# Loading the last head of W_o as sixteen loads of 15, 14, 13 ... 1 partitions instead of one load of 128

## The chip, the cores and the metric

The kernel runs on one NeuronCore of one Trainium2 chip. The metric is the device time of one execution in microseconds (us). The kernel before takes 659.15 us, the median of three runs that lie between 659.08 and 659.29. The profile is of one execution of the same program.

## The reference, cut to what matters

Two blocks follow each other for a batch of B = 2, one token each, width D = 512, in bf16: attention over a cache of 8192 positions with 32 heads of 128, and a gated layer of width F = 1376.

```python
h  = x + A(layernorm(x))          # A: q = x @ wq; softmax(q k^T / sqrt(128)) v; ... @ wo
h2 = h + B(layernorm(h))          # B: relu(x @ W_gate) * (x @ W_up) @ W_down
# k_cache, v_cache: (2, 32, 8192, 128)   wq: (512, 4096)   wo: (4096, 512)
# W_gate, W_up: (512, 1376)   W_down: (1376, 512)
```

The two caches are 256 MiB, the weights about 12 MiB. Each byte is read once and used for little arithmetic.

## The kernel before, in words

The cache is walked in steps of four heads of one batch entry; the last four heads are done in two steps of two heads, called p0 and p1 (in the code `steps[Q+1]` and `steps[Q+2]`). A step loads 8 MiB of keys and 8 MiB of values (half of that in p0 and p1) into three rotating buffers of the on-chip memory, `bufs[0]` to `bufs[2]`, in the trace `tile`. VectorE multiplies the keys by the query and sums them by halves (`products` L375, `scores` L393 and L395), TensorE and ScalarE take a share of the positions (`scores_pe`, L340 to L367, and `act_sums`, L381), and TensorE multiplies the exponentials with the values (`values` L446, `values_cols` L469).

All large loads are issued by SyncE (SP) in the order of the code, which is written out by hand. The tail of that order is: the values of p0; W_o's first set (`load_set(0)`, 2 MiB, L567); the values of p1 (4 MiB, L165); W_o's other three sets (1 MiB, 512 KiB and 256 KiB, L567); W_o's head 30 (128 KiB, L589); W_o's head 31 (128 KiB, L590); W_gate and W_up (1376 KiB each, L612); then W_down in seven loads, three of 32 partitions with 32 KiB each (L616) and four of 128 partitions with 640, 384, 128 and 128 KiB (L621). The last DMA stores the result (L736). Buffer space that a load writes has to be free first, so most issues carry a wait for the engine that read the old contents.

There is a second wait on each issue. The framework gives every DMA one of eight completion counters, in turn, in the order of issue. Before a counter is used again, SP waits until the DMA that used it last has landed completely. As SP issues in order, an issue waits for the DMA eight places before it, and everything behind it in the program of SP waits as well. In the program of the kernel before, the places at the tail are these (the number is the place in SP's own order):

```
34 values p0      35 W_o set 0     36 values p1     37 W_o set 1 (1 MiB)
38 W_o set 2      39 W_o set 3     40 W_o head 30   41 W_o head 31
42 W_gate         43 W_up          44-46 W_down 32-partition loads
47-50 W_down 128-partition loads   51 store
```

So W_gate (42) is issued when the values of p0 (34) have landed, W_up (43) when W_o's set 0 (35) has, the first small load of W_down (44) when the values of p1 (36) have.

After the last scores, TensorE multiplies the heads with W_o (`attend_set` L502; heads 30 and 31 by `attend`, L509), VectorE adds x (L659) and forms the second normalisation (L663 to L677), TensorE multiplies with W_gate and W_up (`through`, L686) and then with W_down (`down`, L719); `down` starts the result from the residual and goes through the eleven chunks of F, each of which needs its part of W_down. VectorE and ScalarE copy the result out (L734, L735), and SP stores it.

The functions that the edit touches:

Of the kernel before, what the change touches and what calls it, by code (L numbers as in the profile page):

```python
# [13 lines left out]
def _free(t, offset, dims):  # L14

    return bass.AP(tensor=t.tensor, offset=t.offset + offset, ap=[t.ap[0]] + [list(d) for d in dims])


def _dram(t, offset, dims):
    return bass.AP(tensor=t.tensor, offset=t.offset + offset, ap=[list(d) for d in dims])  # L20
# [3 lines left out]
def kernel(  # L24
# [13 lines left out]
    nc = tc.nc  # L38
    P = nc.NUM_PARTITIONS
    B, Sq, D = A_x.shape  # L40
    _, Hkv, Sk, Dh = A_k_cache.shape
    Hq = A_wq.shape[1] // Dh
# [26 lines left out]
    HM = 30  # L69
# [55 lines left out]
    wo = bufs[0][:, HALF:TILE]  # L125
# [61 lines left out]
    with tc.manual_schedule():  # L187

        for b, k, n in ((0, 0, 2), (0, 2, 2), (1, 0, 2), (1, 2, 1), (1, 3, 1)):
            nc.scalar.dma_start(  # L190
                out=xr[b:b + 1, k * P:(k + n) * P], in_=_dram(A_x, b * D + k * P, [[D, 1], [1, n * P]]),
# [10 lines left out]
            out=nscale, in_=nscale, compare_op=ALU.not_equal, fill=-SCALE,  # L202
# [5 lines left out]
            out=ident_f, in_=ident_f, compare_op=ALU.not_equal, fill=1.0,  # L208
# [4 lines left out]
            out=sel, in_=sel, compare_op=ALU.not_equal, fill=1.0,  # L213
# [9 lines left out]
            out=pick, in_=pick, compare_op=ALU.not_equal, fill=1.0,  # L223
# [24 lines left out]
        for g0 in range(0, NQ, 4):  # L248
            for n0 in range(NH * g0 * Dh, NH * (g0 + 4) * Dh, 4 * Dh):
                q_ps = ps2.tile([B, 4 * Dh], f32, tag="o")  # L250
                for c in range(KC):
                    nc.tensor.matmul(  # L252
                        out=q_ps, lhsT=xn[:, c, :], rhs=wq_sb[:, c, n0:n0 + 4 * Dh], start=(c == 0), stop=(c == KC - 1),
                    )
                nc.vector.tensor_copy(qrow[:, n0:n0 + 4 * Dh], q_ps)
            for b in range(B):
                r_ps = ps2.tile([P, 4, Dh], f32, tag="tp")
                for j in range(NH):
                    nc.tensor.matmul(
                        out=r_ps[j * (P // NH):(j + 1) * (P // NH)], lhsT=sel[:, b, 0:P // NH],  # L260
# [5 lines left out]
        for j in range(2):  # L266
            nc.tensor.matmul(
                out=r_ps[j * (P // 2):(j + 1) * (P // 2)], lhsT=sel[:, B - 1, :],
# [116 lines left out]
        def scores(s):  # L385

            scol = scols[s.i]
            width = Dh
            while width > 8:
                half = width // 2  # L390
                lo = _free(s.kt, s.na * Dh, [[Dh, s.nv - s.na], [1, half]])
                hi = _free(s.kt, s.na * Dh + half, [[Dh, s.nv - s.na], [1, half]])
                nc.vector.tensor_tensor(out=lo, in0=lo, in1=hi, op=ALU.add)  # L393
                width = half
            nc.vector.tensor_reduce(  # L395
                out=scol[:, s.na:s.nv], in_=_free(s.kt, s.na * Dh, [[Dh, s.nv - s.na], [1, 8]]), axis=AXIS.X, op=ALU.add,
            )
            pms[s.i] = small.tile([P, 1], f32, tag="pm", name="pm", bufs=2)
            nc.vector.tensor_reduce(out=pms[s.i], in_=scol, axis=AXIS.X, op=ALU.max)  # L399
# [187 lines left out]
        for k in range(1, len(SETS)):  # L587
            load_set(k)
        nc.sync.dma_start(out=wo[:, HM * D:(HM + 1) * D], in_=_dram(A_wo, HM * Dh * D, [[D, P], [1, D]]))  # L589
        nc.sync.dma_start(  # L590
            out=wo[:, (HM + 1) * D:Hq * D], in_=_dram(A_wo, (HM + 1) * Dh * D, [[P // 4 * D, 4], [D, P // 4], [1, D]]),
        )
        scores(p0)

        def first():
# [15 lines left out]
        for w, src in ((0, B_W_gate), (1, B_W_up)):  # L611
            nc.sync.dma_start(  # L612
                out=wgu[:, w].rearrange("p c f -> p (c f)"), in_=_dram(src, 0, [[KC * F, P], [1, KC * F]]),
            )
        for q0 in range(AGAIN, P, AGAIN):
            nc.sync.dma_start(  # L616
                out=wd_sb[q0:q0 + AGAIN, FC - 1, :], in_=_dram(B_W_down, (F - P + q0) * D, [[D, AGAIN], [1, D]]),
            )
        for f0, n in FSETS[:-1]:
# [10 lines left out]
            out=z2_ps, lhsT=ones, rhs=_free(zc, ((B - 1) * NQ + groups[Q][1]) * NH, [[1, nb]]), start=True, stop=True,  # L630
# [63 lines left out]
        for c in range(KC):  # L694
            nc.tensor.transpose(hT_ps[:, c, :], hb[:, c].rearrange("p k b -> p (k b)"), ident)
        nc.scalar.activation(
            out=hrow.rearrange("q (p c) -> q p c", c=KC), in_=hT_ps.rearrange("q c p -> q p c"), func=ACT.Copy,
# [9 lines left out]
            out=gate, in0=g_ps, scalar=0.0, in1=_free(rvar, 0, [[0, FC], [1, B]]), op0=ALU.max, op1=ALU.mult,  # L707
# [59 lines left out]
```

## Time and profile before

| what | from | value |
|---|---|---|
| median of three runs | times | 659.15 us (659.08 to 659.29) |
| the profiled execution's span | page | 657.5 us |
| median less span, which the span does not hold | worked out | 1.65 us |
| HBM read | page, part 3 | 281.05 MB, 427 GB/s over the span |
| busy share of VectorE / TensorE / ScalarE | page, part 1 | 85% / 54% / 19% |
| W_gate and W_up issued at | timeline of SP | 624.84 and 629.68 us |
| W_gate, issue to landing | page, part 6 | 22.8 us |
| last load of W_down, issue to landing | page, part 6 | 6.9 us |

The page gives no other time of the profiled execution than its span. Times in the views are counted from the start of the span. A row of SP in the timeline is the issue of a DMA, not its transfer: the transfer lies between the issue and the landing, and may wait behind older transfers. The transfers run on 16 DMA engines, and a DMA has landed when each engine that took part has reported; the trace also holds these reports one by one, and each engine's packets with their sizes and durations.

### The profile page before, as it was taken

To read this page: it belongs to the slowest core of one execution; us is meant where nothing else is said; L and a number is where in the kernel's file an instruction comes from. 1 tells how busy PE (TensorE), PEld (TensorE's weight loads), DVE (VectorE), ACT (ScalarE), POOL (GpSimd) and SP (SyncE) were. 2 spreads that over 40 slices of the span, in tenths; PEclk is the share of its full clock that TensorE was granted. 3 is DMA by queue.
4 is the path that set the end of the run, shared out by engine and by line. 5 is a ranking of instruction groups with operands and counts; after the bars stand their busy time and mean duration, and the time that the engine had idled before them with its cause. 6 is when DMAs were issued, how large, how long until landed. Compare 5 with 4: busy or idle time off the path is not lost.

```text
span 657.5 us, 5117 instructions
## 1 busy us (share of the span) xinstructions
PE 352.1 (54%) x2118; PEld 158.9 (24%) x2118; DVE 558.1 (85%) x252; ACT 123.6 (19%) x337; POOL 24.1 (4%) x36
## 2 busy tenths in 40 slices
PE   0730934809175380926539092552918458291997
PEld 0310311304022130312204031220403224030456
DVE  0599697988979799897979989796997969999982
ACT  0230030200203020030301103030210304201870
POOL 3080000000000000000000000000000000000020
PEclk9975775958778596877959687695968869686895
DMA  9999999999999999999999999999999999999997
GB/s 383 447 444 447 387 440 443 447 399 444 439 443 436 419 436 435 439 439 436 423 443 424 439 440 427 447 416 443 439 423 440 423 443 436 423 444 413 425 425 291
DMA packets 6948, 281.37 MB, mean 428 GB/s; under 512 B 809, under 2 KB 1422, under 8 KB 1934
## 3 DMA queue, kind: packets, MB, share of 16 engines
q1 hardware_dynamic: 6916, 281.06, 99.1%
q8 instruction: 16, 0.26, 0.1%
q14 instruction: 6, 0.05, 0.0%
q10 hardware_dynamic: 10, 0.00, 0.0%
HBM read 281.05 MB, written 0.00 MB: 427 GB/s over the span
## 4 chain that ended last, share of the span: by engine, by line
DVE 42%; DMA 37%; PE 18%; ACT 1%; issue 1%; ACTq 0%; SPq 0%; DVEq 0%
DMA tile<-in_A_k_cache_dram 30%; DVE tile L375 19%; DVE tile L393 18%; PE pv_ps L446 16%; DMA tile<-in_A_wo_dram 4%; DVE scol L395 2%; DMA tile<-in_A_x_dram 2%; DMA tile<-in_B_W_down_dram 1%; PE q_ps L252 1%; DVE pgq L420 1%; ACT ecol L415 1%; DVE pm L399 1%; DVE qrep L395 0%; DVE pm L410 0%; DVE hmax L412 0%
## 5 line engine op out<-in xcount | busy, mean ns | idle before, releaser
L446 PE MATMUL pv_ps<-tile,pgq 128*16 128x512 bf16 x960 | 244.3, 421 | 235.8 <-DVE pgq L420 223.2
L375 DVE TENSOR_TENSOR tile<-tile,qrep 128x29696 bf16<-128x29696 bf16 (+3 forms) x16 | 232.4, 14524 | 44.9 <-DMA tile<-in_A_k_cache_dram 44.9
L393 DVE TENSOR_TENSOR tile<-tile 128x14848 bf16<-128x14848 bf16 (+7 forms) x68 | 236.4, 3477 | 2.2
L446 PEld LDWEIGHTS <-pgq 128*16 128x16 bf16 x960 | 91.6, 97 | 378.1 <-DVE pgq L420 234.5
L451 ACT ACTIVATE pv<-pv_ps 16x512 f32<-16x512 f32 (+1 forms) x16 | 9.4, 589 | 243.7 <-PE pv_ps L446 243.6
L350 ACT ACTIVATE tile<-t_ps 128x1024 bf16<-128x1024 bf16 x53 | 52.6, 1022 | 12.6 <-PE t_ps L349 12.1
L415 ACT ACTIVATE ecol<-scol,nmax 128x256 bf16<-128x256 f32 x14 | 7.1, 508 | 196.1 <-DVE nmax L414 196.1
L340 PE MATMUL row_ps<-tile,qz 128*24 128x512 bf16 (+1 forms) x98 | 30.1, 389 | 18.0 <-ACT tile L350 17.9
L349 PE MATMUL t_ps<-ident,tile 128*128 128x128 bf16 x424 | 32.3, 229 | 13.0 <-DMA tile<-in_A_k_cache_dram 13.0
L349 PEld LDWEIGHTS <-tile 128*128 128x128 bf16 x424 | 25.8, 103 | 28.1 <-issue 14.2
L395 DVE TENSOR_REDUCE scol<-tile 128x232 f32<-128x1856 bf16 (+1 forms) x14 | 28.9, 2067 | 0.5
L641 POOL TENSOR_TENSOR tile<-ident 6x2 bf16<-6x2 bf16 x1 | 2.1, 2147 | 583.5 <-ACT tile L381 583.5
L420 DVE TENSOR_TENSOR pgq<-ecol,ownb 128x1024 bf16<-128x1024 bf16 x15 | 10.4, 692 | 10.3 <-ACT ecol L415 10.3
L381 ACT ACTIVATE tile<-tile 128x128 bf16<-128x128 bf16 x60 | 17.6, 293 | 1.9 <-DVE tile L375 1.9
L281 POOL COPY qzp<-qTs 128x4 bf16<-128x4 bf16 x1 | 15.0, 14982 | 26.1 <-DVE qTs L276 26.1
L375 DVE TENSOR_TENSOR tile<-tile,qpair 128x4096 bf16<-128x4096 bf16 (+3 forms) x4 | 15.5, 3883 | 0.0
L340 PEld LDWEIGHTS <-qz 128*24 128x24 bf16 (+1 forms) x98 | 7.9, 92 | 27.6 <-issue 22.7
L239 DVE CAST xc<-x_ps 128x8 f32<-128x8 bf16 x1 | 0.2, 167 | 15.5 <-PE x_ps L238 15.5
L367 ACT ACTIVATE scol<-sc_ps 32x24 f32<-32x24 f32 (+1 forms) x56 | 11.7, 209 | 7.7 <-PE sc_ps L362 7.2
L362 PE MATMUL sc_ps<-ident_f,tile 24*128 24x24 f32 (+2 forms) x68 | 7.2, 220 | 11.1 <-ACT tile L358 11.1
L358 ACT ACTIVATE tile<-row_ps 24x512 f32<-24x512 f32 (+2 forms) x17 | 10.0, 586 | 13.5 <-PE row_ps L340 13.5
L381 ACT ACTIVATION_READ_ACCUMULATOR tile<-tile 128x1 f32 x60 | 11.2, 186 | 0.0
(133 smaller groups left out, 143.8 us busy)
## 6 DMA issues: line engine op xcount, KB each, us to landing
tile<-in_A_k_cache_dram SPq DMA_DIRECT2D x2, 4096.0 KB
tile<-in_A_v_cache_dram SPq DMA_DIRECT2D x2, 4096.0 KB, 19.6
tile<-in_A_wq_dram SPq DMA_DIRECT2D x1, 4096.0 KB, 12.2
tile<-in_A_wo_dram SPq DMA_DIRECT2D x1, 2048.0 KB
tile<-in_B_W_gate_dram SPq DMA_DIRECT2D x1, 1376.0 KB, 22.8
tile<-in_B_W_up_dram SPq DMA_DIRECT2D x1, 1376.0 KB
tile<-in_A_wo_dram SPq DMA_DIRECT2D x1, 1024.0 KB, 23.8
tile<-in_B_W_down_dram SPq DMA_DIRECT2D x1, 640.0 KB
```

The source lines that it names most:

```text
L281: nc.gpsimd.tensor_copy(qzp[:, :, 6:8], qTs[:, B - 1, Hq - NH:Hq].rearrange("p (k j) -> p k j", j=2),)
L340: nc.tensor.matmul(out=row_ps, lhsT=z, rhs=s.kt[:, (nv + c0 + k) * Dh:(nv + c0 + k + 4) * Dh], start=(u == 0), stop=(u == U - 1),)
L349: nc.tensor.transpose(t_ps[:, k, :], s.kt[:, t * Dh:(t + 1) * Dh], ident)
L350: nc.scalar.activation(out=s.kt[:, (nv + c0) * Dh:(nv + c0 + TPC) * Dh], in_=t_ps.rearrange("p t s -> p (t s)"), func=ACT.Copy,)
L367: nc.scalar.activation(out=scols[s.i][r, nv:s.nt].rearrange("p (u t) -> p t u", t=4), in_=sc_ps[r, :, :, j], func=ACT.Copy,)
L375: nc.vector.tensor_tensor(out=kv, in0=kv, in1=_free(s.qr, 0, [[0, n], [1, Dh]]), op=ALU.mult)
L381: nc.scalar.activation(out=kv, in_=kv, func=ACT.Copy, accum_out=scols[s.i][:, t:t + 1])
L393: nc.vector.tensor_tensor(out=lo, in0=lo, in1=hi, op=ALU.add)
L395: nc.vector.tensor_reduce(out=scol[:, s.na:s.nv], in_=_free(s.kt, s.na * Dh, [[Dh, s.nv - s.na], [1, 8]]), axis=AXIS.X, op=ALU.add,)
L415: nc.scalar.activation(out=ecol, in_=scols[s.i], func=ACT.Exp, scale=SCALE, bias=nmax, accum_out=zs[:, s.b, s.g:s.g + 1],)
L420: nc.vector.tensor_tensor(out=s.pg, in0=_free(ecol, 0, [[VG, s.nt // VG], [0, NH], [1, VG]]), in1=_free(ownb, 0, [[0, s.nt // VG], [VG, NH ...
L446: nc.tensor.matmul(out=pv_ps[s.i][r, :], lhsT=s.pg[:, u].rearrange("p j t -> p (j t)"), rhs=s.vt[:, u * VG * Dh:(u + 1) * VG * Dh], start= ...
```

## The change

The load of W_o's head 31 (place 41) is replaced by a loop of sixteen loads over consecutive partitions: 15, 14, 13, 12, 11, 10, 9, 8, 8, 7, 6, 5, 4, 3, 2 and 1. Together they are the same 128 partitions with 1 KiB each, in the same place. Nothing else is edited.

```diff
         nc.sync.dma_start(out=wo[:, HM * D:(HM + 1) * D], in_=_dram(A_wo, HM * Dh * D, [[D, P], [1, D]]))
-        nc.sync.dma_start(
-            out=wo[:, (HM + 1) * D:Hq * D], in_=_dram(A_wo, (HM + 1) * Dh * D, [[P // 4 * D, 4], [D, P // 4], [1, D]]),
-        )
+        r0 = 0
+        for n in (15, 14, 13, 12, 11, 10, 9, 8, 8, 7, 6, 5, 4, 3, 2, 1):
+            nc.sync.dma_start(
+                out=wo[r0:r0 + n, (HM + 1) * D:Hq * D], in_=_dram(A_wo, ((HM + 1) * Dh + r0) * D, [[D, n], [1, D]]),
+            )
+            r0 += n
+        assert r0 == P
         scores(p0)
```

In SP's program the sixteen loads take the places 41 to 56; W_gate moves from place 42 to 57, W_up from 43 to 58, the seven loads of W_down from 44-50 to 59-65, and the store from 51 to 66. The other engines have the same instructions in the same order as before; on TensorE, the weight load of head 31 now waits for the counters of all the small loads.

## The prediction

> **What bounds the kernel now.** I read the page's slices and queues first, then the chain that ended last, then SP's issues and its waits, because the edit is on SP.
>
> The page's DMA slices and its third part:
>
> ```profile
> DMA  9999999999999999999999999999999999999997
> ...
> q1 hardware_dynamic: 6916, 281.06, 99.1%
> ```
>
> The DMA engines are busy 90% or more in every slice but the last, and SP's queue alone fills 99.1% of their time. The transfers bound the kernel as a whole: any time in which the queue is empty is added, unless it is won back later.
>
> The end of the chain that ended last:
>
> ```profile
> 618.99 24.67 DMA tile<-in_A_wo_dram
> ...
> 644.18 9.77 DMA tile<-in_B_W_down_dram
> 653.94 0.04 issue
> 653.99 0.60 PE d_ps L719 x15
> 654.58 0.03 issue
> 654.61 0.33 PE d_ps L719 x4
> ```
>
> The end hangs on W_down's landing: the last four matmuls start at 654.61. By the engines' reports in the trace, W_down's last load lands at 654.57, which is also its issue at 647.65 plus the page's 6.9. From there 2.97 us remain to the end of the span (657.54): matmuls, copies, the store.
>
> SP's issues in the timeline of the tail:
>
> ```profile
> 617.67 0.33 SPq L165 DMA_DIRECT2D tile<-in_A_v_cache_dram  x1
> 618.05 1.38 SPq L567 DMA_DIRECT2D tile<-in_A_wo_dram  x3
> 619.47 0.43 SPq L589 DMA_DIRECT2D tile<-in_A_wo_dram  x1
> 619.94 0.43 SPq L590 DMA_DIRECT2D tile<-in_A_wo_dram  x1
> 624.84 0.33 SPq L612 DMA_DIRECT2D tile<-in_B_W_gate_dram  x1
> 629.68 0.33 SPq L612 DMA_DIRECT2D tile<-in_B_W_up_dram  x1
> 639.34 4.03 SPq L616 DMA_DIRECT2D tile<-in_B_W_down_dram  x3
> 643.73 4.25 SPq L621 DMA_DIRECT2D tile<-in_B_W_down_dram  x4
> 655.56 0.32 SPq L736 DMA_DIRECT2D out_dram<-tile  x1
> ```
>
> and SP's waits:
>
> ```profile
> SPq L616 <- DMA tile<-in_A_v_cache_dram: 9.3, 1, 9.3
> ...
> SPq L612 <- DMA tile<-in_A_wo_dram: 4.5, 1, 4.5
> SPq L612 <- DMA tile<-in_A_v_cache_dram: 4.4, 1, 4.4
> SPq L616 <- DMA tile<-in_A_wo_dram: 3.0, 2, 2.1
> ```
>
> W_gate and W_up wait for landings of data that they don't use: these are the waits for the DMA eight places before. W_gate still goes out at 624.84, some 20 us before the engines come to it, so the queue never runs dry.
>
> **The change, part by part.**
>
> (1) *W_gate is pushed back.* What is queued on SP behind each new wait is W_gate, W_up, all of W_down. The places follow the rule of eight, and the landings of places 33 to 40 are those of before, since the queues are first in, first out and what is missing stands behind them. Place 41 (15 partitions) goes at 619.94. Place 42 waits for place 34: 624.84, where W_gate was issued. Place 43 waits for 35: 629.68. Place 44 waits for the values of p1: 639.34. Place 45 waits for W_o's set 1: landed 641.82, issued 641.84. Place 46 waits for set 2: 643.06. Place 47 waits for set 3, landed 643.66: 643.68. From here the landings no longer bind (head 30 lands at 643.99, place 41 about then), and the issues go back to back: 48, 49, ... 56, then W_gate at 57, ten steps after 643.68.
>
> (2) *The step.* No row shows a run of SP loads over few partitions. On one side are the five one-partition loads on ScalarE's queue at the start: 213 ns the shortest, 265 ns the median, with some 25 ns between, so 0.29 us a step. On the other side are the runs of 128-partition loads here: 618.99 to 619.47 to 619.94, 0.47 a step. Nearest are SP's own small ones, the 32-partition loads of L616 (0.311 to 0.341) and the two-partition store (0.317); with the 0.045 us between issues they give 0.36, which I take. W_gate is then issued at 643.68 + 10 x 0.36 = 647.3 (646.6 with 0.29; 648.4 with 0.47). That is 22.5 us later than before.
>
> (3) *The queue runs dry.* By the engines' reports head 31 was in between 641.32 (first engine) and 644.32 (last); after that nothing is queued but the few KiB of the new loads, until W_gate. What then has to flow is, for each engine: W_gate 8 packets of 11008 bytes at 0.413 us, W_up the same, W_down 8 x 0.196 + 8 x 0.121 + 22 x 0.046: 10.16 us in all. Before, the last engine took 10.25 us from 644.32 to 654.57. Now it is paid from a standing start. Issue to first packet: 0.75 for the store, 1.04 to 1.84 over the sixteen engines for the first load of the kernel; I take 1.4. Last packet to report: 0.32 (store). Instruction fetches also go over these engines, 0.88 to 1.01 us for 16 KiB in the trace, two of them after 647; if one hits the last engine it adds 0.94, if not, nothing: I take half, 0.5. Sum: landing = W_gate's issue + 1.4 + 10.16 + 0.32 + 0.5 = + 12.4. The lower end is 0.75 + 10.16 + 0.32 = 11.2, the upper 1.84 + 10.16 + 0.32 + 0.94 = 13.3. As a cross-check, the first load took 12.2 from issue to landing with 8 x 1.213 = 9.7 us of packets, an overhead of 2.5; that gives 12.7.
>
> So W_down lands at 647.3 + 12.4 = 659.7 in place of 654.57: +5.1 us. The ends are 646.6 + 11.2 = 657.8 (+3.2) and 648.4 + 13.3 = 661.7 (+7.1). W_down's own issues, seven steps from 648.0, keep ahead of the engines (W_gate and W_up are 6.6 us of packets); its last one waits for W_gate's landing, near 652.5, still ahead.
>
> (4) *Head 31 itself.* The bytes are the same. The one-partition load, place 56, goes at 646.9 and lands 1.15 later (the store: 655.56 to 656.71), at 648.1; TensorE's head 30 and 31 ran at 646.53 before. The sum with x and the normalisation move by some 1.4 us, to about 649.7 for the first W_gate matmul; W_gate's landing near 652.4 covers it. Were that cover gone, the 1.4 us would stand at the end.
>
> (5) *TensorE behind W_gate and W_up.* W_gate's matmuls (1.75) and the normalisation's rest run from 652.4 to about 656; W_up lands near 655.8, its matmuls (1.58) end near 657.5, W_down's 44 matmuls need 1.81: 659.3, within the landing at 659.7. It costs nothing; if W_down came 1 us sooner, TensorE would take half of that back. The 2.97 us behind the landing stay.
>
> (6) *Shares of the engines.* The split gives other numbers of rows to the 16 engines. Whoever had eight rows of head 31 (8 x 0.046 = 0.37 us) can lose at most that or get 0.37 more. Since the engines now drain and wait for W_gate, this is covered by the empty time; without the empty time it would count in full.
>
> By the Trainium skill, DMA: Bandwidth & Descriptors, "Why a DMA increments its semaphore by 16 and not by 1", a load over n < 16 partitions runs on the n lowest engines, so the lowest would get 16 rows and the highest none; the trace before bears out only that a one-partition load reports once. That rule changes (6) by 0.37 at most. The same page's "Rules for kernel authors" says to coalesce small transfers and that under 64 KB mostly overhead is paid, with a fixed part of about 2 us each; it speaks against this change. With eight in flight 2 us would be 0.25 a step, under the 0.36 by which the sum goes; with that alone W_gate would go at 646.2 and the end come 1.1 us sooner, so here issue counts, not latency.
>
> The profiled span would be 657.5 + 5.1 = 662.6. The median lies 1.65 above the span; 659.15 + 5.1 = 664.3.
>
> **The rivals.**
>
> *A costlier step.* The first one-partition load on ScalarE's queue took 0.514 us. If each small load costs that plus the gap, 0.55, W_gate goes at 649.2, W_down lands at 661.6: 666.2. For it speaks that these loads have shapes that the trace before does not hold on SP; against it, that the other four of that run, the store and L616 all stay at or under 0.341.
>
> *One engine does the rows.* If a load whose row count shares no factor with 16 falls to one engine, that engine gets up to 128 rows, 128 x 0.046 = 5.9 us, most of it after 644; it would be through near 650, and W_gate's packets there wait some 1.3 us longer: about 665.8. Nothing in the trace shows it, and 1.3 us is in the upper range.
>
> *Not slower: the standing start evens the engines out.* The first and last engine end 3.0 us apart before (reports 651.57 to 654.57). Starting W_gate together, all would end alike, and half of that could be won. It is part of my sum already. It decides only if W_gate is issued by 654.57 + 1.3 - 11.2 = 644.7 (1.3 us is 0.2%), a step of 0.10 us; the shortest issue in the trace is 0.213. With a step of 0.10 the time would be 659.15 + 1.3 = 660.4 at the lower end of (3). It could also end here if the waits did not bind: if head 31 stayed hidden, the time would lie within 0.37 us of 659.15, by (6). Against that stands that W_gate and W_up are seen waiting 4.4 and 4.5 us at L612 for just such landings.
>
> **How the numbers follow.** My case has 0.80 (664.3, own range 662.4 to 666.3), the costlier step 0.09 (666.2 and up), one engine 0.07 (665.8), not slower 0.04 (659.2). The range 662.4 to 667.0 takes in the first case's ends and the slower rivals. About 0.2%, 1.3 us, is what a measurement of this kernel can tell from no change. Slower by more than that is all but the last case: 0.96. That last splits into 0.03 for the same and 0.01 for faster.
>
> **What would show it.** In the changed profile: issues of the small loads at 624.8, 629.7, 639.3, 641.8, 643.1, 643.7 and then in a row of some 0.36; W_gate's issue at 646.6 to 648.4, and its issue to landing at about 5 us in place of 22.8; DMA share near nothing between 645 and 648.5; TensorE waiting for W_gate at L686; the last landing near 659.7 with 3.0 us behind it. The prediction is wrong if W_gate goes out near 625 (the rule of eight read wrongly), if the row of issues has another step, or if the stream from W_gate to the last landing is not 11 to 13 us.

## The result, and the profile after

The changed kernel takes 665.47 us, the median of four runs (665.27 to 665.94), against 659.12 us before (the median of four; 659.15 is that of three of them): a ratio of 1.0095 with a 95% interval of 1.0083 to 1.0106. That is 6.35 us slower. The profiled execution's span is 663.7 us, 6.2 more than before, and the median lies 1.8 above it.

The page's DMA slices and its third part:

```profile
DMA  9999999999999999999999999999999999999966
...
q1 hardware_dynamic: 7028, 281.06, 98.2%
```

The bytes are the same. The last two slices are no longer full, and SP's queue has fallen from 99.1% to 98.2% of a longer span. In the windows of the tail one sees where (each row is a stretch of 2 us; the last two columns are the DMA share and GB/s):

```profile
642.00:644.00 2.00, 1.75 (x50) 1.67 (x49) 0.59 (x3) 0.00 (x0) 0.00 (x0) 0.50 0.33 115
644.00:646.00 2.00, 2.00 (x70) 2.00 (x68) 0.16 (x1) 0.00 (x0) 0.00 (x0) 0.50 0.12 27
646.00:648.00 2.00, 0.62 (x19) 0.54 (x17) 0.00 (x0) 0.00 (x0) 0.00 (x0) 0.50 0.23 41
648.00:650.00 2.00, 0.87 (x6) 0.72 (x6) 0.69 (x6) 0.00 (x0) 0.00 (x0) 0.50 0.78 297
```

From 642 to 648 the DMA engines were a third busy at most, where the kernel before moved more than 400 GB/s. SP's issues in the timeline of the tail say why (start, duration up to the end of the last issue of the row, what was issued, how many):

```profile
618.80 0.43 SPq L589 DMA_DIRECT2D tile<-in_A_wo_dram  x1
619.28 27.52 SPq L592 DMA_DIRECT2D tile<-in_A_wo_dram  x16
646.90 0.36 SPq L616 DMA_DIRECT2D tile<-in_B_W_gate_dram  x1
647.36 0.38 SPq L616 DMA_DIRECT2D tile<-in_B_W_up_dram  x1
647.83 1.43 SPq L620 DMA_DIRECT2D tile<-in_B_W_down_dram  x3
649.35 3.53 SPq L625 DMA_DIRECT2D tile<-in_B_W_down_dram  x4
```

The sixteen small loads hold SP's order from 619.28 to 646.8, and W_gate goes out 22.06 us later than before. SP's waits name what held it there (us in total, times, longest):

```profile
SPq L592 <- DMA tile<-in_A_v_cache_dram: 14.3, 2, 9.3
...
SPq L592 <- DMA tile<-in_A_wo_dram: 8.0, 4, 4.5
```

These are the waits that stood at W_gate, W_up and the small loads of W_down before (4.4, 4.5, 9.3 and 3.0, and 0.3 at L621). In sum they are 14.3 and 8.0 us in place of 13.7 and 7.8, about what they were; they have moved to instructions ahead of W_gate. The chain that ended last (start, duration, what) runs through the issues themselves:

```profile
646.25 0.25 SPq L592
646.51 0.04 issue
646.55 0.25 SPq L592
646.80 0.05 issue
646.87 0.03 issue
646.90 0.36 SPq L616
...
649.83 10.25 DMA tile<-in_B_W_down_dram
660.08 0.04 issue
660.12 0.59 PE d_ps L723 x11
660.72 0.03 issue
660.75 0.33 PE d_ps L723 x4
```

Before, this stretch of the chain was two pieces of DMA with 0.5 us of SP's issues between them (643.66 to 644.18). Now SP's issue time is on the path, then the transfer from a standing start, then the same end. W_down's last load lands at 660.71 by the engines' reports, 6.14 later than before, and 3.04 remain behind it (2.97 before). TensorE waits for each of the three weights in turn (in brackets the idle time before the row and what ended it):

```profile
648.24 0.27 PE L509 MATMUL att_ps<-ocol,tile 128*128 128x2 bf16 x4 [1.62 <-DMA tile<-in_A_wo_dram]
...
652.58 1.58 PE L690 MATMUL g_ps<-hn,tile 128*128 128x2 bf16 x44 [3.21 <-DMA tile<-in_B_W_gate_dram]
...
656.43 1.58 PE L690 MATMUL u_ps<-hn,tile 128*128 128x2 bf16 x44 [1.23 <-DMA tile<-in_B_W_up_dram]
...
659.18 1.84 PE L723 MATMUL d_ps<-tile,hm 128*2 128x128 bf16 x44 [0.97 <-DMA tile<-in_B_W_down_dram]
```

Head 31 is late too (1.62 us at L509), but its lateness is covered by W_gate's.

### The profile page after: what moved, and what is told of

Same layout as the page of the kernel before. It is cut to its first block, busy times and chain, and to the rows that moved or that the text cites. A ratio compares the mean times of both kernels' runs of the same rounds, so it can differ in the third digit from the quotient of the medians.

```text
span 663.7 us, 5136 instructions
## 1 busy us (share of the span) xinstructions
PE 348.9 (53%) x2118; PEld 157.7 (24%) x2118; DVE 558.1 (84%) x252; ACT 123.4 (19%) x337; POOL 24.3 (4%) x36
## 3 DMA queue, kind: packets, MB, share of 16 engines
q1 hardware_dynamic: 7028, 281.06, 98.2%
## 4 chain that ended last, share of the span: by engine, by line
DVE 42%; DMA 37%; PE 18%; SPq 1%; issue 1%; ACT 1%; ACTq 0%; DVEq 0%
DMA tile<-in_A_k_cache_dram 29%; DVE tile L375 19%; DVE tile L393 18%; PE pv_ps L446 16%; DMA tile<-in_A_wo_dram 4%; DVE scol L395 2%; DMA tile<-in_A_x_dram 2%; DMA tile<-in_B_W_down_dram 2%; PE q_ps L252 2%; DVE pgq L420 1%; ACT ecol L415 1%; DVE pm L399 1%; SPq L592 0%; DVE qrep L395 0%; DVE pm L410 0%
## 5 line engine op out<-in xcount | busy, mean ns | idle before, releaser
L446 PE MATMUL pv_ps<-tile,pgq 128*16 128x512 bf16 x960 | 240.4, 416 | 237.2 <-DVE pgq L420 225.3
L420 DVE TENSOR_TENSOR pgq<-ecol,ownb 128x1024 bf16<-128x1024 bf16 x15 | 10.4, 692 | 10.2 <-ACT ecol L415 10.2
```

Of the source, the lines that this page charges most:

```text
L420: nc.vector.tensor_tensor(out=s.pg, in0=_free(ecol, 0, [[VG, s.nt // VG], [0, NH], [1, VG]]), in1=_free(ownb, 0, [[0, s.nt // VG], [VG, NH ...
L446: nc.tensor.matmul(out=pv_ps[s.i][r, :], lhsT=s.pg[:, u].rearrange("p j t -> p (j t)"), rhs=s.vt[:, u * VG * Dh:(u + 1) * VG * Dh], start= ...
```

## The experiments

Two theories were set against each other. A: the rule of eight pushes W_gate back, the queue runs dry, and the price is that of a late W_gate. B: sixteen small loads cost their time wherever they stand, by packets, reports and uneven shares of the engines. A third, C, blamed the shapes: falling and odd row counts.

**The same sixteen loads on GpSimd's queue.**

```diff
-            nc.sync.dma_start(
+            nc.gpsimd.dma_start(
                 out=wo[r0:r0 + n, (HM + 1) * D:Hq * D], in_=_dram(A_wo, ((HM + 1) * Dh + r0) * D, [[D, n], [1, D]]),
             )
```

> The same sixteen loads (15, 14 ... 1 partitions), issued on GpSimd's queue instead of SP's. They then use other completion counters, and W_gate stands at place 41 of SP's order. Theory A (the counters' rule of eight on SP pushes W_gate back, the queue runs dry): W_gate is issued before 625 us, the stream never stops, the time is that of the kernel before, 659.1 to 659.8 us. Rival B (sixteen small loads cost their time wherever they are issued, through packets, reports and the uneven shares of the engines; 6.35 us for fifteen more loads, 0.42 each): 665.5 us or more.

Measured: 661.09 us (660.56 to 661.43), ratio 1.0027, interval 1.0017 to 1.0037. SP's timeline of this kernel:

```profile
618.14 0.43 SPq L589 DMA_DIRECT2D tile<-in_A_wo_dram  x1
620.04 0.33 SPq L616 DMA_DIRECT2D tile<-in_B_W_gate_dram  x1
626.02 0.33 SPq L616 DMA_DIRECT2D tile<-in_B_W_up_dram  x1
```

W_gate is early again, the queue stays full, and 4.4 of the 6.35 us are gone. B as stated is refuted: the same sixteen loads did not keep their price. But A's 659.1 to 659.8 is missed as well, by 1.3 us. These loads were issued from 562 to 600 us, among the large ones, with 369 more packets under 512 bytes than before (1178 against 809), and the keys of p0 landed at 606.64 in place of 605.43: most of the 1.4 us by which this span is longer is there already, 40 us ahead of the tail. GpSimd issues them in another way (0.52 us each, on a queue of its own), so this remainder is not shown to be that of small loads on SP.

**Four loads of 32 partitions, and eight of 16.**

```diff
-        for n in (15, 14, 13, 12, 11, 10, 9, 8, 8, 7, 6, 5, 4, 3, 2, 1):
+        for n in (32,) * 4:
```

The kernel with eight has `(16,) * 8` in its place.

> Head 31 by four loads of 32 partitions on SP. Theory A: W_gate stands at place 45 and waits for W_o's set 1, so it is issued at 641.7 us; the last engines are still at work on older data until 644.3, the first ones wait some 1.5 us that they had to spare; time 659.1 to 659.8 us. Rival B (0.42 us for each added load): 3 x 0.42 = 1.3 us more, 660.4 us.

> Head 31 by eight loads of 16 partitions on SP. Theory A: W_gate stands at place 49, behind the back-to-back row that starts at 643.6, so it is issued at 644.25 us, 2.65 us sooner than with sixteen loads; with the stream of 12.4 us that the prediction took it ends 2.1 us later than before (661.2), with the 13.8 us that the changed kernel showed 3.5 us later (662.6). I take 662.0 us. Rival B: 7 x 0.42 = 3.0 us more, 662.1 us; this run alone does not tell A from B, it gives the size of the stream's term.

Measured: four loads 660.90 us (660.64 to 661.31), ratio 1.0026 (1.0017 to 1.0036); eight loads 663.82 us (663.46 to 664.10), ratio 1.0069 (1.0054 to 1.0084). SP's timelines, first of the kernel with four:

```profile
619.96 19.31 SPq L592 DMA_DIRECT2D tile<-in_A_wo_dram  x4
641.64 0.35 SPq L616 DMA_DIRECT2D tile<-in_B_W_gate_dram  x1
```

and of the kernel with eight:

```profile
619.05 25.25 SPq L592 DMA_DIRECT2D tile<-in_A_wo_dram  x8
644.39 1.08 SPq L616 DMA_DIRECT2D tile<-in_B_W_gate_dram  x1
```

W_gate goes out where theory A put it (641.7 and 644.25), so the rule of eight is right to 0.14 us. The prices are higher than A's: 1.8 us with four, where A had at most 0.7, and 4.7 with eight, where I took 2.9. With eight, W_gate's own issue took 1.08 us in place of 0.33, and the last landing came 14.6 us after its start. With four, the engines' reports show half of the price. Before, W_gate lands on the first engine at 644.59 and on the last at 647.63; with four loads the two are 647.03 and 647.41. The first engines lost 2.4 us and the last none, which is harmless by itself. But W_up then lands on fifteen engines between 650.34 and 650.92 and on the sixteenth at 652.20, and this gap stays to the end: the last landing is at 655.49, 0.9 later than before. So the engines' even start makes a single straggler the last one. With the engines 3 us apart before, the last group alone set the end. From the last landing to the end it took 3.28 us in place of 2.97. The profiled execution is the fastest of its ten (660.64), and its span is 1.2 longer than before; what the other executions lose beyond that is not resolved.

**Sixteen loads of 8 partitions.**

```diff
-        for n in (15, 14, 13, 12, 11, 10, 9, 8, 8, 7, 6, 5, 4, 3, 2, 1):
+        for n in (8,) * 16:
```

> Head 31 by sixteen loads of 8 partitions each on SP: the same number of loads and places as the change, but equal and even shapes, so that no engine gets a share by a falling row count. Theory A: the issues decide, a step of 0.33 us, W_gate issued at 646.9 to 647.1 us, time 665.5 us within 0.5. Rival C (the uneven shapes or the odd row counts cost the time): clearly less, 663 us or below.

Measured: 666.08 us (665.82 to 666.67), ratio 1.0105 (1.0089 to 1.0120). C is refuted: even shapes are no faster. The time lies 0.1 us above A's range and 0.6 above the change; the 95% intervals of the two ratios overlap. The profiled execution is the slowest of the four (666.67), and its chain has one slow issue:

```profile
643.77 1.29 SPq L592
645.06 0.04 issue
645.10 0.29 SPq L592
645.40 0.04 issue
645.44 0.30 SPq L592
```

This issue took 1.0 us more than its neighbours, and W_gate went out at 647.87, 0.97 later than in the changed kernel. Whether the other three executions had such an issue is not recorded, so it is not shown to be the 0.6 us between the medians. A fetch of 16 KB of instructions went over a DMA engine from 643.8 to 644.7. In the kernel with eight loads, W_gate's issue of 1.08 us stood beside such a fetch at 644.1 too; in the changed kernel a fetch at 644.2 delayed no issue. That the fetch holds the issue is a guess.

**W_gate late, with head 31 in one load.** These kernels leave head 31 as it was, and hold the loads of W_gate, W_up and W_down behind a tiny VectorE write.

```diff
-        for w, src in ((0, B_W_gate), (1, B_W_up)):
...
         normalise(Q + 2)
+        nc.vector.memset(wgu[:, 0, 0, 0:2], 0.0)
+        for w, src in ((0, B_W_gate), (1, B_W_up)):
...
```

> Head 31 stays one load, as before. Instead, W_gate, W_up and W_down are issued late: a tiny VectorE write into W_gate's place, behind the last normalisation (near 645.0 us), has to come first (the value written is overwritten by the load). No small loads at all. Theory A: what costs is the late issue; W_gate goes out near 645.1 us, the stream from its issue to the last landing takes 13.8 us as in the changed kernel, then 2.95 to the end: span 661.9, time 663.5 us (1.8 us less than the change, whose W_gate goes 1.8 us later). Rival B (the small loads themselves cost): 659.1 us.

Here the write stands behind `normalise(Q + 2)`. Measured: 663.53 us (663.17 to 663.64), ratio 1.0063 (1.0048 to 1.0078). SP's timeline:

```profile
619.16 0.43 SPq L590 DMA_DIRECT2D tile<-in_A_wo_dram  x1
644.87 0.33 SPq L643 DMA_DIRECT2D tile<-in_B_W_gate_dram  x1
645.29 0.43 SPq L643 DMA_DIRECT2D tile<-in_B_W_up_dram  x1
```

Without one added small load, a W_gate that is issued at 644.87 costs 4.3 us; the last landing is at 658.43, 13.56 after the issue, against 13.81 in the changed kernel. The changed kernel's W_gate goes 2.03 us later and its median is 1.94 higher. That is the mechanism of the result, reproduced without its trigger.

> As the run before, with the tiny VectorE write put between two earlier copies, so that W_gate goes out near 641.7 us, where it went with four loads of 32 partitions. At that moment the first engines have just run out of work and the last ones have 2.5 us left. If the 1.8 us of the run with four loads came from the late issue (the engines start W_gate's end together and lose the spread of 3 us, so that one engine with an instruction fetch is last), this run takes the same, 660.9 us. If they came from the four loads themselves, it takes 659.1 to 659.4 us.

Here the write stands behind the first of the three `lay_rows`, and W_gate goes out at 641.48:

```profile
641.48 0.33 SPq L639 DMA_DIRECT2D tile<-in_B_W_gate_dram  x1
```

Measured: 660.22 us (660.07 to 660.82), ratio 1.0014 (1.0005 to 1.0024). That is between the two forecasts: 1.0 us of the 1.8 of the run with four loads comes with the late issue alone. The reports have the same form as there (W_gate 646.54 to 647.53, W_up 649.82 to 652.33, the end 655.54). The other 0.8 us are left to the four loads, or to scatter that this comparison can't resolve.

**Three loads.**

```diff
-        for n in (15, 14, 13, 12, 11, 10, 9, 8, 8, 7, 6, 5, 4, 3, 2, 1):
+        for n in (48, 48, 32):
```

> Head 31 by three loads of 48, 48 and 32 partitions. W_gate stands at place 44 and waits for the values of p1, so it goes out at 639.3 us, while every engine still has more than 1.5 us of older work. Theory A: no engine runs out, 659.1 to 659.5 us. Rival B (0.42 us for each added load, or 0.6 as four loads would have it): 660.0 us or more.

Measured: 659.94 us (659.55 to 660.21), ratio 1.0009 (0.9999 to 1.0019). W_gate went out at 639.59:

```profile
639.59 0.35 SPq L616 DMA_DIRECT2D tile<-in_B_W_gate_dram  x1
```

No engine ran out of work (W_gate's reports lie from 645.34 to 648.19, nearly as far apart as before), and the difference can't be told from none. Its middle, 0.7 us, is nearer to B's 660.0 than to A's 659.5, so a small price of each of the two added loads (0.35 us at the middle, 0.6 at the upper end of the interval) is neither shown nor excluded by these times. The profile speaks against it: the last engine reports head 30, which stands ahead of the three loads, at 644.76 in place of 643.99, and the end of W_down at 655.21 in place of 654.57, so this execution was 0.77 us behind before the first of them and 0.64 at the end. With sixteen loads on SP the price of each can't be near 0.35 us: against the kernel with the write behind `normalise(Q + 2)`, which has none of them, W_gate goes 2.03 us later and the time is 1.94 higher, which leaves nothing for the loads themselves that could be told from scatter.

## Why the prediction was right

It gave 664.3 us in a range of 662.4 to 667.0; 665.47 came. The sum was +5.1 us, the median moved by 6.35, and the mechanism is the one forecast. One of the prediction's own signs of being wrong did come, though: the stream from W_gate to the last landing is not 11 to 13 us but 13.81. The time stayed inside the range all the same, as W_gate went out 0.4 us sooner than was taken and the range had room for a dearer step. By its steps:

(1) *W_gate is pushed back.* Right. The small loads went at 624.73, 629.57, 639.22, 641.66, 642.97 and 643.60, and then in a row.

(2) *The step.* 0.36 us was taken, 0.33 came (643.60 to 646.90 in ten steps; the single issues take 0.25 to 0.29 with 0.04 between). The row of ScalarE's one-partition loads (0.29) and SP's two-partition store (0.36) bracketed it. W_gate was issued at 646.90 in place of 647.3: 0.4 us less than forecast.

(3) *The queue runs dry.* Right in kind, and the term that was mis-sized. From W_gate's issue to the last landing it took 13.81 us; 12.4 was taken, with an upper end of 13.3. On fifteen of the engines it was 12.1 to 12.6: the last reports are 658.98 for the first and 659.53 for the fifteenth. The sixteenth reported at 660.71. W_down's packets of 5120 bytes all begin by 657.35, but for two at 657.82 and 658.35, and a fetch of 16 KB of instructions ran from 656.8 for 1.07 us. I had put half a fetch (0.5) into the sum; the even start makes its whole length, and a little more, count: the sixteenth report is 1.17 us behind the fifteenth. The packets carry no engine's number, so that the fetch and the late report share an engine is argued from these times. The standing start itself was also dearer than 1.4 us: W_gate's first packets started 0.98 to 1.73 after the issue, as the first load of the kernel had it, but then took 0.47 to 1.43 us each where a packet in the stream takes 0.413.

(4) *Head 31.* The last small load went at 646.55 and landed at 647.78 (forecast: 646.9 and 648.1), and TensorE ran head 31 at 648.24. It is covered by W_gate, as said.

(5) *TensorE behind the weights.* Right: it waits for all three, and 3.04 us stay behind the last landing.

(6) *Shares of the engines.* Without effect here, as said: even shapes are no faster. By the Trainium skill, DMA: Bandwidth & Descriptors, "Why a DMA increments its semaphore by 16 and not by 1", a load over n < 16 partitions runs on the n lowest engines and the issuing engine writes the missing counts at once. The trace agrees in the numbers: the load of 15 partitions left fifteen reports from 640.80 to 644.04, and one at 619.89, when none of its data could have come. That the engines are the lowest ones, no run here shows.

The fixed part of about 2 us, which the prediction takes from the Trainium skill, stands on the same page (DMA: Bandwidth & Descriptors) under "Anatomy of one DMA — SWDGE (gpsimd) path", for loads that GpSimd issues, and not under "Rules for kernel authors". The small loads on SP show less: the one-partition load landed 1.23 us after its issue.

The rivals: the costlier step didn't come (no issue of the change but the first, which waited for nothing and was ahead of time, was over 0.32). One engine did not do the rows (15, 14, 13 ... reports each). The standing start evened the engines out, as the third rival said, and that was worth nothing: what the last engines win, a single straggler takes back.

## What to carry to other kernels

Count the places in a queue, not only the bytes: where each issue waits for the one eight places before, a few extra small loads in front of a large one make the large one wait for landings that it has nothing to do with. Look in SP's timeline for how early the next large load goes out compared with when the engines come to it; here W_gate was issued at 624.84 and its first packet started at 640.97, a lead of 16 us (not the 20 that the prediction says). Two more places cost nothing that could be told from scatter, three cost 1.8 us, seven 4.7. A load that is issued after its queue has run dry costs the whole stream again from a standing start: 13.6 to 14.6 us here for three weights whose packets are 10.2.

## What was not expected

The sixteen engines drift apart step by step, and the steps come with instruction fetches. In the kernel before, the first two large loads report within 0.60 us each. A fetch of 16 KB of instructions follows at 36.8 us, and in the next load fifteen engines report within 0.42 us and the sixteenth at 2.04. After the second such fetch (94.8) two engines are late, after one of 8 KB (111.9) three. In all nine profiles none, one, two and three engines report over 0.9 us behind the first at the second, third, sixth and seventh load. From the third load on the reports spread over some 1.7 us until 420 us into the run, and over some 3 us from 440 on, behind a fetch at 439.4: the next load's last report stands at 3.36, the one before it at 1.65. Packets of a size mostly take the same time (11008 bytes: 0.413 us, the shortest and the median alike): a late engine is behind, not slower, and as long as its queue is full it stays behind. The packets carry no engine's number, so that the late engine is the one that carried the fetch is argued from this count.

Which engines are late can be seen in part. In the kernel with sixteen loads of 8 partitions, head 30, on all engines, reports in groups at 640.60 to 641.02, 641.92 to 642.41 and 643.34 to 643.74; the first load of 8 partitions, right behind it, reports at 640.79 to 641.22 and 642.12 to 642.59, and has no late group. By the rule cited in (6) those are the lowest eight engines; then the late ones are all among the other eight. In the changed kernel the load of 15 partitions lacks one of the early reports, so the sixteenth engine is an early one. Why the latest ones all lie among the upper eight is open; nothing here tried it.

An empty queue makes the engines start together, and then one engine that falls back with an instruction fetch of about 1 us decides the end. In the changed kernel, with eight loads, with sixteen of 8 partitions and in both kernels with W_gate late, the last report is 1.1 to 1.4 us behind the fifteenth, each time behind a fetch during W_up or W_down (656.8, 655.1, 657.5, 654.5 and 647.5). With the engines spread over 3 us before, the same fetches at 647.4 and 652.7 did not make a straggler behind the last group: W_up's reports spread by 3.43 us and W_down's by 3.00.
